# Band attention and a gated product: where P is transposed, and how two heads' scores are written

## The chip, the cores and the metric

The kernel runs on one core of one Trainium2 chip. The metric is the device time of one launch in microseconds (us), the median of a few runs.

## The reference, cut to what matters

Attention has 8 batches of 8 heads (64 heads, numbered n = 0 to 63 through all batches), each with 512 local and 32 global tokens of width 64. A local token sees the global tokens and the local ones within 32 places; a global token sees all.

```python
k_all = concatenate([k_g, k_l]); v_all = concatenate([v_g, v_l])
out_g = sm(scale * q_g @ k_all.T) @ v_all
s_ll  = where(|i - j| <= 32, scale * q_l @ k_l.T, -1e9)
out_l = sm(concatenate([scale * q_l @ k_g.T, s_ll])) @ v_all
x     = concatenate([out_g, out_l]) as (8 * 544, 512)
h     = (x @ w1) * (x @ w2)
out   = (h @ w3) @ w_out
```

All of it is float32. w3 @ w_out is folded into one matrix before it is used.

## The kernel before

**Two ways to multiply.** TensorE takes a float32 product either *plain*, in one matmul instruction that the trace shows as two records, or *split*: both operands are cut into a high part and a low part of type float32r, and two or three matmuls of those are added. Casts to high parts are made on ScalarE (ACT), the differences that give low parts on VectorE (DVE) or GpSimd (POOL). The big products (`first`, lines 816 to 818, and `second`, lines 848 to 850) are split throughout.

**A head.** Four blocks of 128 queries are taken against windows of 192 or 256 keys. `scores` (line 527) writes the four blocks into one PSUM tile `s` of two banks. `minus_max` (line 549) reads it on DVE, adds the mask and finds the maxima; `exps` on ACT makes the weights P in SBUF (two tiles, `P0` and `P1`). For the product with v, P is needed transposed, in the tile `PT` (own blocks of 128 keys, and pieces of the neighbouring blocks) and the tile `G` (global keys). `values` (line 650) then makes eight or more matmuls into two PSUM tiles, `cb` and `u` take the result out, and per pair of heads the rows are divided by their sums and become a part `x` of the rows of the big products.

**Where heads differ.** Heads 0 to 7 (`n < H`) are plain: TensorE transposes P in seven matmuls (lines 583 and 588), and the pieces are copied from PSUM. From head 8 on `PT` and `G` hold high and low parts. TensorE transposes only the four own blocks (line 583) into a PSUM tile, from which ACT takes the high parts and DVE the low. The 32-column edges and the global columns are transposed by DVE (`turn`, line 590, into `TT`), split there, and brought to their partitions by DMA: `move_edges` (lines 605 and 606, SBUF to SBUF into `PT`), `move_out` (line 611, to DRAM) and `move_in` (line 616, back into `G`). `PT` and `G` are single tiles, so these DMAs of a head start only when the values of the head before are done. Scores are plain up to head 15 (`NS = 16`): one step a head, on the 64 partitions that its half of the pair's q and k lie on. From head 16 they are split: q's two parts lie on the two halves of the partitions and k is loaded twice (lines 419 and 420), so that eight matmuls on all 128 partitions (line 546) make one head. The casts and differences for that are `prep_k` and `prep_q`.

**PSUM** has eight banks: `s` two (one buffer, also used by the global scores `sg` and the global transposes `tg`), `t0`, `t1`, `a` and `b` one each, `acc` two.

**What sets the order.** Every step has a cost by engine and a due time; the due times are the numbers of `DUE` (line 70), one a step, in the order in which the steps are listed. `list_schedule` (line 240) goes through a model of time and gives each free engine the ready step that is due first; the program is written in the order that comes out, and each engine then runs its instructions strictly in that order. All DMAs are issued by one queue, SyncE (SP), in order. `tile_orders` (line 1010) says which step must have left a buffer before the next takes it. In the middle of the program, TensorE's steps of a head stand among the matmuls of `first` and `second`, which belong to the batch before.

Of the kernel before, what the change touches and what calls it, by code (L numbers as in the profile page):

```python
# [7 lines left out]
F32 = mybir.dt.float32  # L8
# [22 lines left out]
def i(ap):  # L31
# [3 lines left out]
NX, NO, NK, NQ, MA, NS = (5, 6), 3, 3, 2, 4, 16  # L35
# [10 lines left out]
    scores32=1650, values32=(1180, 1130), gscores32=930, take=(446, 521),  # L46
# [272 lines left out]
def band_attention_glu_kernel(  # L319
# [16 lines left out]

    nc = tc.nc  # L340
    B, H = q_t.shape[0], q_t.shape[1]
    NP = H // 2
    NH = B * H
    TG = 32 * B
    S = 544

    const = ctx.enter_context(tc.tile_pool(name="const", bufs=1))
    p1 = ctx.enter_context(tc.tile_pool(name="p1", bufs=1))
# [49 lines left out]
    def load_q(n):  # L398
        b, h = divmod(n, H)
        qr = p2.tile([128, 512], F32, tag="qr", name=f"qr{n}", bufs=NQ)[0:64]  # L400
        nc.sync.dma_start(qr, q_t[b, h])
        T["qr", n] = qr
# [1074 lines left out]
```

## Time and profile before

| | |
|---|---|
| median of 3 runs | 848.13 us (847.5 to 849.35) |
| span of the profiled execution, first to last instruction | 848.0 us |
| TensorE busy | 833.2 us, 98% of the span |
| DVE, ACT, POOL busy | 67%, 63%, 45% |
| DMA engines busy | 50.1%, 129 GB/s |
| granted TensorE clock, mean | 0.996 of full speed |

The profile is of one execution of 848.0 us, 0.13 us under the median. A matmul's record reaches from its start to the end of its passage, and records overlap, so that what a step takes from TensorE is read from start to start.

### The profile page before, as it was taken

To read this page: it belongs to the slowest core of one execution; us is meant where nothing else is said; L and a number is where in the kernel's file an instruction comes from. 1 tells how busy PE (TensorE), PEld (TensorE's weight loads), DVE (VectorE), ACT (ScalarE), POOL (GpSimd) and SP (SyncE) were. 2 spreads that over 40 slices of the span, in tenths; PEclk is the share of its full clock that TensorE was granted. 3 is DMA by queue.
4 is the path that set the end of the run, shared out by engine and by line. 5 is a ranking of instruction groups with operands and counts; after the bars stand their busy time and mean duration, and the time that the engine had idled before them with its cause. 6 is when DMAs were issued, how large, how long until landed. Compare 5 with 4: busy or idle time off the path is not lost.

```text
span 848.0 us, 17752 instructions
## 1 busy us (share of the span) xinstructions
PE 833.2 (98%) x5818; PEld 750.2 (88%) x5818; DVE 567.0 (67%) x1499; ACT 536.0 (63%) x1445; POOL 383.4 (45%) x477
## 2 busy tenths in 40 slices
PE   7999999899999999999999999999999999999998
PEld 4756679799999999999999999999989999999997
DVE  5677777867777786877787767776877778531111
ACT  4666776765767786867666768676767767521111
POOL 1201455534638474747563645654755656310000
PEclk8999999999999999999999999999999999999999
DMA  9787656554647464746554554645555644200000
GB/s 292 228 250 229 183 165 165 144 129 104 147 94 170 114 158 109 170 104 165 114 137 118 131 142 121 140 116 143 123 136 123 146 97 117 50 26 2 26 18 33
DMA packets 194372, 109.75 MB, mean 129 GB/s; under 512 B 150056, under 2 KB 158504, under 8 KB 194280
## 3 DMA queue, kind: packets, MB, share of 16 engines
q1 hardware_dynamic: 194280, 108.61, 50.1%
q8 instruction: 46, 0.75, 0.4%
q14 instruction: 46, 0.38, 0.2%
HBM read 85.52 MB, written 20.28 MB: 125 GB/s over the span
## 4 chain that ended last, share of the span: by engine, by line
PE 75%; DMA 3%; SPq 1%; ACT 0%; issue 0%; POOL 0%; DVE 0%; ACTq 0%; POOLq 0%
PE acc L848 7%; PE acc L849 7%; PE ap L816 7%; PE acc L850 7%; PE bp L816 7%; PE bp L817 6%; PE ap L817 6%; PE bp L818 6%; PE ap L818 6%; PE av L665 5%; PE s L546 5%; PE t L583 3%; DMA G<-gd 2%; PE av L659 2%; PE sg L715 1%; PE s L539 1%
## 5 line engine op out<-in xcount | busy, mean ns | idle before, releaser
L816 PE MATMUL ap<-x,w12h 128*128 128x256 f32 x544 | 153.8, 283 | 0.0
L816 PE MATMUL bp<-x,w12h 128*128 128x256 f32 x544 | 153.0, 281 | 0.0
L817 PE MATMUL bp<-x,w12h 128*128 128x256 f32 x544 | 151.1, 278 | 0.0
L817 PE MATMUL ap<-x,w12h 128*128 128x256 f32 x544 | 151.0, 278 | 0.0
L818 PE MATMUL bp<-x,w12l 128*128 128x256 f32 x544 | 151.0, 278 | 0.0
L818 PE MATMUL ap<-x,w12l 128*128 128x256 f32 x544 | 150.9, 277 | 0.0
L554 ACT ACTIVATE P<-P,small 128x256 f32<-128x256 f32 (+1 forms) x256 | 121.5, 476 | 19.0 <-DVE small L550 18.7
L550 DVE CUSTOM_DVE_ANT_0 P<-s,cs 128x192 f32<-128x192 f32 (+1 forms) x256 | 88.3, 383 | 25.8 <-PE s L546 16.5
L816 PEld LDWEIGHTS ap<-x,w12h 128*128 128x128 f32 x544 | 102.3, 188 | 2.1 <-issue 0.4
L817 PEld LDWEIGHTS bp<-x,w12h 128*128 128x128 f32 x544 | 102.5, 188 | 1.1
L817 PEld LDWEIGHTS ap<-x,w12h 128*128 128x128 f32 x544 | 102.5, 188 | 1.1
L816 PEld LDWEIGHTS bp<-x,w12h 128*128 128x128 f32 x544 | 102.2, 188 | 1.4 <-issue 0.2
L818 PEld LDWEIGHTS bp<-x,w12l 128*128 128x128 f32 x544 | 102.6, 189 | 0.0
L818 PEld LDWEIGHTS ap<-x,w12l 128*128 128x128 f32 x544 | 102.4, 188 | 0.0
L679 DVE TENSOR_TENSOR u<-av,cb 64x352 f32<-64x352 f32 x112 | 57.5, 519 | 27.1 <-ACT cb L462 25.2
L465 POOL TENSOR_TENSOR kl<-kr,kh 128x608 fp32r<-128x608 f32 x37 | 56.5, 1527 | 36.9 <-ACT kh L462 26.6
L665 PE MATMUL av<-PT,vs 128*128 128x192 f32 x448 | 61.4, 263 | 0.0
L950 PE MATMUL w<-wo,w3f 128*128 128x512 f32 x128 | 60.2, 604 | 0.0
L462 ACT COPY cb<-av 64x352 f32<-64x352 f32 x93 | 41.6, 447 | 27.2 <-PE av L665 25.9
L665 PEld LDWEIGHTS av<-PT,vs 128*128 128x128 f32 x448 | 52.4, 162 | 0.7
L465 POOL TENSOR_TENSOR qs<-qr,qs 64x512 fp32r<-64x512 f32 x31 | 42.4, 1368 | 17.6 <-issue 9.3
L554 ACT ACTIVATION_READ_ACCUMULATOR P<-P,small 128x1 f32 x256 | 48.1, 188 | 0.0
(811 smaller groups left out, 2137.9 us busy)
## 6 DMA issues: line engine op xcount, KB each, us to landing
kr<-in_kd_t_dram SPq DMA_DIRECT2D x96, 152.0 KB, 3.0
raw_w<-in_w_t_dram SPq DMA_DIRECT2D x24, 512.0 KB, 4.9
kpr<-in_kp_t_dram SPq DMA_DIRECT2D x32, 272.0 KB, 3.2
out_dram<-o_None SPq DMA_DIRECT2D x33, 256.0 KB, 2.8
R<-rd SPq DMA_DIRECT2D x64, 128.0 KB, 3.2
gd<-TT SPq DMA_DIRECT2D x112, 64.0 KB, 2.7
vr<-in_v_t_dram SPq DMA_DIRECT2D x28, 256.0 KB, 3.2
G<-gd SPq DMA_DIRECT2D x112, 64.0 KB, 2.7
```

The lines of the kernel that those rows point to most:

```text
L465: (eng or nc.gpsimd).tensor_sub(dst, src, f(hi))
L550: nc.vector.tensor_tensor_reduce(blk(n, e), T["st", n][:, e, 0 : WIN[e][1]], masks[e], -0.125, 3.0e38, ALU.add, ALU.min, T["mn", n][:, e : ...
L554: nc.scalar.activation(blk(n, e), blk(n, e), AF.Exp, bias=T["mn", n][:, e : e + 1], scale=-1.0, accum_out=T["sm", n // 2][:, n % 2, e : e ...
L665: nc.tensor.matmul(av[0:r, o : o + 32 * (s1 - s0)], v[:, 0:r], PT[:, s0:s1, y, j], start=False, stop=(j % 2 == 1 and (plain or y == 1)), s ...
L679: nc.vector.tensor_add(T["u", n // 2][r : r + 64, x], T.pop(("av", n, x))[r : r + 64, 0:352], T["cb", n][r : r + 64, x])
L816: nc.tensor.matmul(d, wh[:, k, c, :], x[:, 0, 0:w], start=(k == m % 2 == 0), stop=False, skip_group_check=True)
L817: nc.tensor.matmul(d, wh[:, k, c, :], x[:, 1, 0:w], start=False, stop=False, skip_group_check=True)
L818: nc.tensor.matmul(d, wl[:, k, c, :], x[:, 0, 0:w], start=False, stop=(k == 3), skip_group_check=True)
L848: nc.tensor.matmul(a, gh[:, m % 2, sl], wh[:, c], start=(m == 0), stop=False, **part)
L849: nc.tensor.matmul(a, gh[:, m % 2, sl], wl[:, c], start=False, stop=False, **part)
L850: nc.tensor.matmul(a, gl[:, m % 2, sl], wh[:, c], start=False, stop=(m in (5, 7)), **part)
L950: nc.tensor.matmul(T["w34", t], T["w3f", t, j // 4][:, j % 4], T["wo"][:, j], start=(j == 0), stop=(j == 7))
```

## The change

Three things change, and with them every number of `DUE` (listed nowhere here).

1. Heads 8 to 15 become plain (`NF = 16` takes the place of `H` in the tests): seven TensorE transposes, plain values, no `turn` and no edge DMAs. Their global v rows lie in the plain `PT` beside those of batch 0.
2. From head 16 the four own blocks no longer pass TensorE. DVE transposes them in 32-by-32 squares (`turn_own`) into `tw`, one DMA writes that to DRAM, and four DMAs read it back into `own`, square by square in its place. The high and low parts are then made from `own`, which is in SBUF, so POOL can make them too.
3. From head 8 on the scores of a pair are one step, plain: for each block first the even head on partitions 0 to 63, then the odd one on 64 to 127, into two PSUM tiles of two banks. Within a tile the even head has one bank and the odd head the other. `load_k`, `load_q`, `prep_k` and `prep_q` are gone; k and q are loaded once a pair.

In PSUM the tags `s`, `t0` and `t1` give way to one tag `pu` with two buffers of two banks, which transposes, scores, values (from head 8), `sg` and `tg` take in turn.

```diff
     def scores(m):
+        q, k = T["q2", m], T["k2", m]
+        for h in range(2):
+            st = T["st", m, h] = ps_1.tile([128, 2, 512], F32, tag="pu", name=f"s{m}_{h}", bufs=2)
+            for e in (2 * h, 2 * h + 1):
+                o, w = WIN[e]
+                for x in range(2):
+                    r, c = slice(64 * x, 64 * x + 64), 256 * (e % 2)
+                    nc.tensor.matmul(st[:, x, c : c + w], q[r, 128 * e : 128 * e + 128], k[r, o : o + w],
+                                     start=(e % 2 == 0), stop=True, skip_group_check=True)
...
+    def turn_own(n):
+        P = Ps[n % NP_][:]
+        t = T["tw", n] = p1.tile([128, 512], F32, tag="tw", name=f"tw{n}")
+        nc.vector.transpose(view(t[:], 0, [32, 4], [128, 4], [1, 32]), view(P, 0, [256, 4], [32, 4], [1, 32]))
+
+    def own_out(n):
+        D = T["od", n] = dram.tile([128, 4, 128], F32, tag="od", name=f"od{n}", bufs=3)
+        nc.sync.dma_start(D, T.pop(("tw", n)).rearrange("p (b x) -> p b x", b=4))
+
+    def own_in(n):
+        D = T.pop(("od", n)).rearrange("(a k) b x -> b k a x", a=4)
+        L = T["own", n] = p1.tile([128, 512], F32, tag="own", name=f"own{n}")
+        for b in range(4):
+            nc.sync.dma_start(L[32 * b : 32 * b + 32].rearrange("k (a x) -> k a x", a=4), D[b])
...
     def pieces(n, e):
-        plain = n < H
+        plain = n < NF
...
+        if not plain:
+            return T["own", n].rearrange("p (a x) -> p a x", a=4), *(PT[:, 2:6, y].rearrange("p a j q -> p a (j q)") for y in range(2))
...
     def values(n, x):
-        plain = n < H
+        plain = n < NF
...
-        av = T["av", n, x] = ps_1.tile([128, 512], F32, tag="ab"[x] if plain else f"t{x}", name=f"av{x}_{n}")
+        if n < H:
+            av = ps_1.tile([128, 512], F32, tag="ab"[x], name=f"av{x}_{n}")
+        else:
+            if x == 0:
+                T["av2", n] = ps_1.tile([128, 2, 512], F32, tag="pu", name=f"av{n}", bufs=2)
+            av = T["av2", n][:, x]
...
     def tile_orders():
+        def take_s(m):
+            for h in range(2):
+                take("pu", 2, ("s", m, h), ("sp", m))
...
             else:
                 take("TT", 1, ("TT", n), ("turn", n))
+                take("own", 1, ("own", n), ("oi", n))
+                take("tw", 1, ("tw", n), ("own", n))
+                if n % 2 == 0 and n + 2 < NH:
+                    take_s(n // 2 + 1)
+                take("pu", 2, ("av", n), ("av", n, 0))
```

**The order, TensorE, scores in the middle of the program.** `s27` are the scores of head 27, `t0_26` the own transposes of head 26, `ap`, `bp` and `acc` the big products. Before:

```order
L818 MATMUL bp2_0_4_4011<-x2_3_0_3747,w12l5_998 128x256
L583 MATMUL t0_26_4076<-cs_78,P0_79 128x128 x4
L546 MATMUL s27_4081<-kh27_3877,qs27_3882 128x192
L546 MATMUL s27_4081<-kl27_3907,qs27_3882 128x192
L546 MATMUL s27_4081<-kh27_3877,qs27_3882 128x256
L546 MATMUL s27_4081<-kl27_3907,qs27_3882 128x256
L546 MATMUL s27_4081<-kh27_3877,qs27_3882 128x256
L546 MATMUL s27_4081<-kl27_3907,qs27_3882 128x256
L546 MATMUL s27_4081<-kh27_3877,qs27_3882 128x192
L546 MATMUL s27_4081<-kl27_3907,qs27_3882 128x192
L816 MATMUL ap2_0_6_4094<-x2_0_0_2765,w12h6_999 128x256
```

With the change, heads 30 and 31 (pair 15):

```order
L844 MATMUL acc2_0_128_3765<-w34h2_559,gl__3899 128x512
L515 MATMUL s15_0_3982<-kq15_3405,qp15_3408 128x192 x2
L515 MATMUL s15_0_3982<-kq15_3405,qp15_3408 128x256 x2
L515 MATMUL s15_1_3987<-kq15_3405,qp15_3408 128x256 x2
L515 MATMUL s15_1_3987<-kq15_3405,qp15_3408 128x192 x2
L810 MATMUL ap2_0_6_4003<-x2_0_0_2441,w12h6_1057 128x256
```

Eight split matmuls a head have become eight plain ones a pair, with the two heads of a block next to each other, and the own transposes are gone from TensorE.

**The order, SP, the DMAs of head 29.** `gd29` is the edge tile on its way through DRAM, `G` and `PT` what the values wait for, `od` and `own` the own blocks, `kq`, `qp`, `vr`, `kpr` loads for later heads. Before:

```order
L611 DMA gd29_4505<-TT_81 128x4x32 x2
L863 DMA out_0_dram<-o2_0_0_None_4503 128x512
L863 DMA out_0_dram<-o2_0_128_None_4508 128x512
L456 DMA vgr4_4529<-in_vg_t_dram 32x512
L457 DMA vgr4_4529<-in_vg_t_dram 32x512
L605 DMA PT1_1050<-TT_81 32x2x96
L606 DMA PT1_1050<-TT_81 32x2x96
L616 DMA G1_1045<-gd29_4505 32x16x32 x2
```

With the change:

```order
L597 DMA gd29_4048<-TT_81 128x4x32 x2
L781 DMA TGr7_4063<-gg7_3992 32x4x128 x4
L782 DMA TGg7_4064<-gg7_3992 32x4x32
L399 DMA kq17_4107<-in_kd_t_dram 128x608
L410 DMA vr15_4109<-in_v_t_dram 128x512
L416 DMA kpr17_4112<-in_kp_t_dram 128x544
L574 DMA od30_4138<-tw30_4127 128x512
L539 DMA rd15_4149<-sums_84 128x2x4
L602 DMA G1_2059<-gd29_4048 32x16x32 x2
L591 DMA PT1_2031<-TT_81 32x2x96
L592 DMA PT1_2031<-TT_81 32x2x96
L580 DMA own30_4200<-od30_4138 32x4x128 x4
```

The four DMAs on which the values of head 29 wait still stand together; more of SP's work stands between them and the edge tile's way out, and five DMAs a head (`od` and four `own`) are new.

**The order, TensorE, the first steps.** `idle` are matmuls without a use. Before:

```order
L396 MATMUL idle1_103<-vgs_82 128x256
L707 MATMUL sg0_151<-kpr0_116,QG0_112 128x272 x2
L396 MATMUL idle0_102<-vgs_82 128x256 x2
L539 MATMUL s0_170<-kq0_129,qp0_127 128x192
L539 MATMUL s0_170<-kq0_129,qp0_127 128x256 x2
L539 MATMUL s0_170<-kq0_129,qp0_127 128x192
L707 MATMUL sg1_188<-kpr1_140,QG0_112 128x272 x2
L950 MATMUL w34_0_196<-wo_99,w3f0_0_146 128x512
```

With the change:

```order
L388 MATMUL idle1_103<-vgs_82 128x256
L500 MATMUL s0_142<-kq0_114,qp0_116 128x192
L500 MATMUL s0_142<-kq0_114,qp0_116 128x256 x2
L500 MATMUL s0_142<-kq0_114,qp0_116 128x192
L701 MATMUL sg0_176<-kpr0_137,QG0_112 128x272 x2
L388 MATMUL idle0_102<-vgs_82 128x256 x2
L701 MATMUL sg1_191<-kpr1_128,QG0_112 128x272 x2
L944 MATMUL w34_0_197<-wo_99,w3f0_0_165 128x512
```

The first head's scores now stand ahead of the global ones, and the two no longer share one buffer.

## Rows read from the trace of the kernel before

**Rows 1.** The page, busy time and share of the span by engine.

```profile
PE 833.2 (98%) x5818; PEld 750.2 (88%) x5818; DVE 567.0 (67%) x1499; ACT 536.0 (63%) x1445; POOL 383.4 (45%) x477
```

**Rows 2.** Waits of PE: total us, times, longest us.

```profile
PE s L539 <- DVE small L734: 3.4, 2, 1.9
PE av L659 <- DMA G<-gd: 2.4, 6, 0.8
PE sg L707 <- DMA kpr<-in_kp_t_dram: 2.0, 1, 2.0
```

**Rows 3.** Timeline of PE, heads with split values: start us, us, what.

```profile
310.55 0.28 PE L818 MATMUL ap<-x,w12l 128*128 128x256 f32 x1
310.66 0.29 PE L659 MATMUL av<-G,vgs 128*128 128x288 f32 x1
...
311.72 0.30 PE L816 MATMUL ap<-x,w12h 128*128 128x256 f32 x1
...
313.01 0.28 PE L818 MATMUL ap<-x,w12l 128*128 128x256 f32 x1
313.12 0.25 PE L546 MATMUL s<-kh,qs 128*128 128x192 f32 x1
...
314.02 0.30 PE L816 MATMUL ap<-x,w12h 128*128 128x256 f32 x1
314.16 0.28 PE L817 MATMUL ap<-x,w12h 128*128 128x256 f32 x1
...
315.30 0.28 PE L818 MATMUL ap<-x,w12l 128*128 128x256 f32 x1
315.41 0.60 PE L583 MATMUL t<-cs,P 128*128 128x128 f32 x4
315.76 0.36 PE L816 MATMUL bp<-x,w12h 128*128 128x256 f32 x1
315.97 0.28 PE L817 MATMUL bp<-x,w12h 128*128 128x256 f32 x1
```

**Rows 4.** Timeline of PE, plain scores of one head.

```profile
124.10 0.28 PE L818 MATMUL ap<-x,w12l 128*128 128x256 f32 x1
124.31 1.78 PE L539 MATMUL s<-kq,qp 64*128 64x192 f32 x8
126.02 0.39 PE L816 MATMUL bp<-x,w12h 128*128 128x256 f32 x1
126.24 0.28 PE L817 MATMUL bp<-x,w12h 128*128 128x256 f32 x1
```

**Rows 5.** Timeline of PE, plain values and plain transposes of one head.

```profile
91.95 0.65 PE L659 MATMUL av<-G,PT 128*128 128x288 f32 x2
...
94.27 1.88 PE L950 MATMUL w<-wo,w3f 128*128 128x512 f32 x4
95.99 0.60 PE L583 MATMUL t<-cs,P 128*128 128x128 f32 x4
...
96.75 1.02 PE L950 MATMUL w<-wo,w3f 128*128 128x512 f32 x2
```

**Rows 6.** Timeline of PEld: weight loads of the first, useless matmuls.

```profile
1.18 2.21 PEld L396 LDWEIGHTS idle<-vgs 128*128 128x128 f32 x6 [1.18 <-DVE vgs L393]
4.04 1.36 PEld L396 LDWEIGHTS idle<-vgs 64*128 64x128 f32 x8 [0.65 <-issue]
```

**Rows 7.** Instructions of tile G: duration ns min/median/max, first and last start us.

```profile
L616 SPq DMA_DIRECT2D G<-gd x112: 318/479/1077, 123.6 to 739.1; - x112
...
DMA to landing us min/median/max: 2.1/2.7/5.0
```

**Rows 8.** The same of tile TT, the two edge DMAs into PT.

```profile
L605 SPq DMA_DIRECT2D PT<-TT x56: 597/643/1437, 122.2 to 737.0; - x56
L606 SPq DMA_DIRECT2D PT<-TT x56: 585/628/1171, 122.9 to 737.7; - x56
```

**Rows 9.** Groups by line, DVE: the maxima, busy us, mean ns, idle before.

```profile
L550 DVE CUSTOM_DVE_ANT_0 P<-s,cs 128x192 f32<-128x192 f32 (+1 forms) x256 | 88.3, 383 | 25.8 <-PE s L546 16.5 <-PE s L539 8.4
```

More of the change, by code (lines that the diff above doesn't have):

```diff
@@ L342, in band_attention_glu_kernel @@
     NP = H // 2
+    PB = 2
+    NF = PB * H
     NH = B * H
@@ L360, in band_attention_glu_kernel @@
     masks = [cs[:, 384:576], mask, mask, mask[:, 0:192]]
-    Ps = [const.tile([128, PW], F32, tag=f"P{e}", name=f"P{e}") for e in range(2)]
+    Ps = [const.tile([128, PW], F32, tag=f"P{e}", name=f"P{e}") for e in range(NP_)]
     TT = const.tile([128, 2, 352], F32R, tag="TT", name="TT")
@@ L524, in blk @@
     def blk(n, e):
-        return Ps[n % 2][:, PAT[e] : PAT[e] + WIN[e][1]]
-    def scores(n):
-        st = ps_1.tile([128, 4, 256], F32, tag="s", name=f"s{n}")
-        T["st", n] = st
-        T["mn", n] = minima()[:, 4 * (n % 2) : 4 * (n % 2) + 4]
-        if n % 2 == 0:
-            T["sm", n // 2] = sums[:, n // 2 % 2]
-        if n < NS:
-            rows = slice(64 * (n % 2), 64 * (n % 2) + 64)
-            q, k = T["q2", n // 2][rows], T["k2", n // 2][rows]
-            for e in range(4):
-                o, w = WIN[e]
-                nc.tensor.matmul(st[:, e, 0:w], q[:, 128 * e : 128 * e + 128], k[:, o : o + w], start=(e % 2 == 0),
-                                 stop=True, skip_group_check=True)
-            return
-        qs, kh, kl = T.pop(("qs", n)), T.pop(("kh", n)), T.pop(("kl", n))
+        return Ps[n % NP_][:, PAT[e] : PAT[e] + WIN[e][1]]
@@ L543, in scores, with scores1 @@
+    def scores1(n):
+        m, x = divmod(n, 2)
+        T["mn", n] = minima()[:, 4 * x : 4 * x + 4]
+        if x == 0:
+            T["sm", m] = sums[:, m % 2]
+        st = T["st", n] = ps_1.tile([128, 4, 256], F32, tag="pu", name=f"s{n}", bufs=2)
+        r = slice(64 * x, 64 * x + 64)
+        q, k = T["q2", m][r], T["k2", m][r]
         for e in range(4):
             o, w = WIN[e]
-            for j, kk in enumerate((kh, kl)):
-                nc.tensor.matmul(st[:, e, 0:w], qs[:, 128 * e : 128 * e + 128], kk[:, o : o + w],
-                                 start=(j == e % 2 == 0), stop=(j == 1), skip_group_check=True)
@@ L549, in minus_max, with scores @@
-    def minus_max(n, e):
-        nc.vector.tensor_tensor_reduce(blk(n, e), T["st", n][:, e, 0 : WIN[e][1]], masks[e], -0.125, 3.0e38,
+            nc.tensor.matmul(st[:, e, 0:w], q[:, 128 * e : 128 * e + 128], k[:, o : o + w], start=(e % 2 == 0),
+                             stop=True, skip_group_check=True)
+    def scores(m):
+        for x in range(2):
+            c = 4 * x
+            T["mn", 2 * m + x] = minima()[:, c : c + 4]
+        T["sm", m] = sums[:, m % 2]
+        q, k = T["q2", m], T["k2", m]
[3 more added lines that the diff above has]
+                o, w = WIN[e]
+                for x in range(2):
+                    r, c = slice(64 * x, 64 * x + 64), 256 * (e % 2)
+                    nc.tensor.matmul(st[:, x, c : c + w], q[r, 128 * e : 128 * e + 128], k[r, o : o + w],
+                                     start=(e % 2 == 0), stop=True, skip_group_check=True)
@@ L1043, in tile_orders @@
                         take("cb", 1, ("cg", k[1]), ("cg", k[1]))
[L1044 to L1047 removed]
+            take("P", NP_, ("P", n), ("mmax", n, 0))
     tile_orders()
@@ L1087, in head @@
         done = [("exps", n, e) for e in range(4)]
-        add(("t", n), only("PE", COST["transposes" if n < H else "own"]), t, done, transposes, n)
-        read(("t", n), ("P", n))
-        free = [("av", n - 1, x) for x in range(2)] if n % H or n > H else [("clear", x, b) for x in ("PT", "G")]
+        if n < NF:
+            add(("t", n), only("PE", COST["transposes"]), t, done, transposes, n)
+            read(("t", n), ("P", n))
+        free = [("av", n - 1, x) for x in range(2)] if n not in (0, NF) else [("clear", x, int(n > 0)) for x in ("PT", "G")]
@@ L1091, in head @@
         last = []
         for e, d in zip((0, 1, 2, 3, 6, 4, 5), (0.9, 1.0, 1.7, 1.3, 1.1, 1.5, 1.6)):
-            if n >= H and e in (1, 2, 3, 6):
+            if n >= NF and e in (1, 2, 3, 6):
                 continue
             h, l = ("hi", n, e), ("lo", n, e)
-            src = [("t", n)] if e not in (4, 5) else [("gw", n // 4, e - 4) if n < H else ("tgi", n // 4)]
-            add(h, hi(COST["hi"][e], 128) if e == 4 else only("ACT", COST["hi"][e]) if e == 5 else hi_psum(COST["hi"][e], COST["hi_dve"][e]), t + d, src + free, weights_hi, n, e, eng=True)
+            src = [("t", n) if n < NF else ("oi", n)] if e not in (4, 5) else [("gw", n // 4, e - 4) if n < H else ("tgi", n // 4)]
@@ L1098, in head @@
+            own = n >= NF and e == 0
+            add(h, hi(COST["hi"][e], 128) if e == 4 else only("ACT", COST["hi"][e]) if e == 5 else hi(COST["hi"][e], 512) if own else hi_psum(COST["hi"][e], COST["hi_dve"][e]), t + d, src + free, weights_hi, n, e, eng=True)
             d += 0.8
-            tile_ = ("TG", n // 4) if e in (4, 5) else (f"t{int(e > 0)}", n)
+            tile_ = ("TG", n // 4) if e in (4, 5) else ("own", n) if own else ("t", n)
             read(h, tile_)
-            if e not in (4, 5):
-                held[h] = tile_
@@ L1103, in head @@
-            if n >= H:
-                add(l, either(None, (COST["lo"][e], COST["lo"][e])) if e else only("DVE", COST["lo"][e]), t + d, [h], weights_lo, n, e, eng=True)
+            if e not in (4, 5) and not own:
+                held[h] = (f"t{int(e > 0)}", n)
+            if n >= NF:
+                add(l, either(None, (COST["lo"][e], COST["lo"][e]) if e else COST["ownl"]), t + d, [h], weights_lo, n, e, eng=True)
                 read(l, tile_)
-                if e == 0:
-                    held[l] = tile_
@@ L1108, in head @@
-            last.append(l if n >= H else h)
-        if n >= H:
+            last.append(l if n >= NF else h)
+        if n >= NF:
             add(("turn", n), only("DVE", COST["turn"]), t, [*done, ("clear", "vgs")], turn, n)
             read(("turn", n), ("P", n))
+            add(("own", n), only("DVE", COST["ownt"]), t + 0.2, done, turn_own, n)
+            read(("own", n), ("P", n))
+            add(("oo", n), dma(450), t + 1.0, [("own", n)], own_out, n, nbytes=262144)
+            read(("oo", n), ("tw", n))
+            add(("oi", n), dma(450, 450, 450, 450), t + 3.0, [("oo", n)], own_in, n, nbytes=300000)
@@ L1131, in head @@
                     [me, *[("sum", n, 0)] * x], values_take, n, x, eng=True)
-                read(("sum", n, x), (f"av{x}", n), ("u", n // 2))
+                read(("sum", n, x), (f"av{x}", n) if n < H else ("av", n), ("u", n // 2))
                 continue
@@ L1163, in pair_values @@
         take("vr", 1, ("vr", m), ("load", "v", m))
-        add(("load", "v", m), dma(450, *[450] * (m < NP)), t - 14.0, (), load_pair, m, nbytes=262144)
-        if m < NP:
+        add(("load", "v", m), dma(450, *[450] * (m < PB * NP)), t - 14.0, (), load_pair, m, nbytes=262144)
+        if m < PB * NP:
             return
@@ L1235, in batch @@
             add(("load", "qg", 0), dma(650, 650), t - 45.0, [("clear", "QG", 0)], load_qg0, nbytes=65536)
-            add(("load", "vg", 0), dma(650), t - 12.0, [("clear", "PT", 0)], load_vg0, nbytes=65536)
-            read(("load", "vg", 0), ("PT", 0))
+            for c in range(PB):
+                add(("load", "vg", c), dma(650), t - 12.0 + 40.0 * c, [("clear", "PT", 0)], load_vg0, c, nbytes=65536)
+                read(("load", "vg", c), ("PT", 0))
             read(("load", "qg", 0), ("QG", 0))
@@ L1376, in band_attention_glu_kernel @@
         for b in range(2):
-            add(("clear", x, b), only("POOL", ns), base(H) - (30.0 if x == "QG" else 6.0) if b else due, (), fresh, x, b)
+            add(("clear", x, b), only("POOL", ns), (base(H) - 30.0 if x == "QG" else base(NF) - 6.0) if b else due, (), fresh, x, b)
     add(("clear", "vgs"), only("POOL", 952), 0.0, (), fresh_vgs)
```

168 lines of the change are left out of this document (73 added, 95 removed), and 322 rows, old and new, of the table DUE.

## The prediction

> **What bounds the kernel now.** I read the page first: TensorE is busy in 98% of the span, DVE, the next, in 67% [rows 1]. Then the waits of TensorE: they come to less than 10 us in all, most of it before the first heads have their data (the scores of the first heads wait 3.4 us for the maxima that free their PSUM tile, the global scores 2.0 us for their keys), and 2.4 us in six waits later, where values wait for the edge tile G [rows 2]. So the kernel is as long as TensorE's list of work. What a step adds to that list I read in the timeline from start to start, since a record's length overlaps the next.
>
> Between products of the big matrices, two slots of which take 0.23 us, the own transposes of a head cost 315.97 - 315.30 - 0.23 = 0.44 us; they include a later start of the product behind them [rows 3]. The split scores of a head cost 314.16 - 313.01 - 0.23 = 0.92 us, the split values 311.72 - 310.55 - 0.11 = 1.06 us [rows 3]. The plain scores of one head cost 126.24 - 124.10 - 0.23 = 1.91 us, of which 1.71 us are the matmuls and 0.2 us the slots at both sides [rows 4]. The plain values cost 94.27 - 91.95 = 2.32 us and the seven plain transposes 96.75 - 95.99 = 0.76 us [rows 5]; to the latter I add the 0.09 us by which transposes delay a product (0.21 instead of 0.11 to 0.12 us behind them [rows 3]), 0.85 us.
>
> **The change part by part.**
>
> *Heads 8 to 15 plain.* Transposes 8 x (0.85 - 0.44) = +3.3 us; values 8 x (2.32 - 1.06) = +10.1 us. Against that, their eight steps of scores at 1.91 us go: -15.3 us. The edges' transposes on DVE, their casts and the edge DMAs of eight heads go too. They lie beside TensorE's work and I cost their going at nothing.
>
> *Own blocks off TensorE, heads 16 to 63.* 48 x 0.44 = -21.1 us. Instead DVE gets a third transpose a head and SP five DMAs. DVE is idle in a third of the span [rows 1] and loses all its low parts of k and q, ACT loses 96 casts and the low parts of the own blocks may go to POOL. So these engines end up with no more work than before, and I cost it at nothing on the path. The cover is the distance between a pair's scores and its values: in the new order there are two heads' values and some 20 us of TensorE's work between them. If that were short, the values would be late instead.
>
> *Scores of a pair in one plain step, heads 8 to 63.* The split scores of heads 16 to 63 go: 48 x 0.92 = -44.2 us. There come 28 steps at a price p that the trace does not show. If the two heads of a block, on the two halves of the partitions, run beside each other, a step takes what one head takes: p = 1.91 us [rows 4]. If one head runs after the other, p = 2 x 1.71 + 0.2 = 3.6 us. The nearest row is that of the matmuls without a use at the start: eight weight loads on half the partitions, with the halves in turn, take 1.36 us together, six loads on all partitions 2.21 us [rows 6]. One after the other at the latter pace the eight would take 2.9 us; so the halves go side by side there. That stretch runs at a slower pace than the later ones (2.21 / 6 = 0.37 us a load, where two products with their loads take 0.23 us), so that later the instructions come faster one behind the other; for this I add 0.1 us and take p = 2.0: +56.0 us. All above but the 28 steps is 3.3 + 10.1 - 15.3 - 21.1 - 44.2 = -67.2 us; with them it is -11.2 us. With p = 1.91 it is -13.7, with p = 3.6 it is +33.6; the sum is zero at p = 2.4.
>
> The Trainium skill (TensorE: Matmul & The Clock Gate, Measured speedup) gives less than full gain for packed rows: 3.07 times for four row tiles. An estimate by that page, the same 77% of the ideal for two, would give p = 2 x 1.71 / 1.53 + 0.2 = 2.4 us and a sum of about zero. By that page nothing would be left of the saving; the row above shows no such loss, at its slower pace, and no row here shows it at the later one.
>
> *The new place of the scores in PSUM.* A pair's scores take both buffers of `pu`, and the values of the next head need one of them, which is free when four maxima are taken. A maximum is 0.38 us [rows 9], four of them 1.5 us; the new order leaves about 5 us of products or more behind the scores in the middle of the program. I cost it at nothing, as long as DVE takes the maxima at once.
>
> *The start.* The first scores no longer wait for the tile of the global ones. At most the 3.4 + 2.0 us of the two waits go [rows 2]; but the fold products behind need their weights, which come by the same queue in nearly the same order, so I take -1 us, between -5 and +2.
>
> *The edges.* The values of a head wait for four DMAs that may start only when the values of the head before are done. With medians: two into PT, 0.64 + 0.63 us of issue, two into G, 2 x 0.48 us, small gaps, and 2.7 us to landing, 5.1 us in all (4.5 us with the fastest landing) [rows 7, 8]. From the new order, with a product counted as 0.115 us and one of `second` as 0.23 us, the work between the values of two heads is 4.5 us twice (heads 29 and 45), 5.1, 5.2 and 5.4 us once, and 5.9 or 6.1 us eight times; before the change it was 6.3 us and more but for one place at the end. So two or three heads wait about 0.6 us, and spread adds some: +1.5 us to the waits of 2.4 us that there are [rows 2].
>
> *Sum.* -11.2 - 1 + 1.5 = -10.7 us against the 848.0 us of the profiled execution: **837.3 us**. The median of the runs shown is 0.13 us above it; I predict **837.4 us**.
>
> **The rivals.**
>
> *A. The edges come too late: slower.* Per head, five DMAs come to SP and about two go, for 1.5 us more of issue at half a microsecond each; and more of them stand ahead of the edges in the queue, which is strictly in order. If SP comes to the first edge DMA L us after the values' end, the chain of 5.1 us becomes 5.1 + L; for the 13 heads with 6.1 us or less (72.1 us together) the waits are 13 x (5.1 + L) - 72.1. At L = 2 they are 20 us: 848.0 - 11.2 - 1 + 20.2 = **856 us**. It decides from L = 1.4, where the saving is eaten. For it: the six waits for G show that this chain touches TensorE already [rows 2]. Against: the low parts of k and q, on which loads in the same queue waited, are gone, and at the tight places the four DMAs stand together in the new order.
>
> *B. The halves run beside each other in part or not at all: no gain, or much slower.* With half of the overlap p is (1.91 + 3.6) / 2 = 2.75 us, the sum -67.2 + 28 x 2.75 = +9.8 us and the time 848.0 + 9.8 + 0.5 = **858 us**; with none it is 848.0 + 33.6 + 0.5 = **882 us**. For it stands only that no row shows a pair at the later pace; against it the weight loads [rows 6]. The Trainium skill's figure above would stand between, at about 848 us.
>
> *C. The waits move into PSUM's two buffers.* If each of the 24 pairs' next values waits 0.45 us for the maxima, 10.8 us are given back: **848 us**, no change. For it: the maxima had 25.8 us of idle time before them, mostly for scores, so DVE follows scores closely only when it is not behind with other work [rows 9]. Against: 5 us against 1.5 us.
>
> *D. More than forecast.* p at its lower bound, the start's two waits gone, no more waits at the edges: -13.7 - 5 = **829 us**.
>
> **How the numbers follow.** The forecast case (830 to 846 us, with p from 1.9 to 2.2 and waits up to some 5 us) gets 0.72, A 0.10, B 0.05, C 0.08, D 0.05. About 0.2% (1.7 us) is what a measurement of this kernel tells from no change. Faster by more: the forecast and D, 0.77. Within it: most of C and a little of A and B, 0.09. Slower: the rest, 0.14. The range takes in D below and the first part of A above, so far that no more than 2 in 10 is outside: 828 to 852 us.
>
> **What would show it.** In the profile of the changed kernel, right: no transposes of own blocks on TensorE from head 16; a pair's scores taking 1.8 to 2.0 us from the last product before to the first behind; values of heads 8 to 15 at 2.3 us; TensorE's busy share still about 98%, with waits for G below 5 us. Wrong: pairs of 2.4 us or more (B); a row of waits of PE for G or PT in total over 12 us (A), or for the maxima on scores, values and `sg` (C); DVE's or SP's chain of waits in the middle of the program.

## The result, and the profile after

The changed kernel takes **839.12 us** (median of 4 runs, 836.66 to 840.28) against 847.82 us (847.42 to 849.35) of the kernel before on the same chip: ratio 0.989, with a 95% interval of 0.9869 to 0.9912. Forecast were 837.4 us, between 828 and 852. The profiled execution has a span of 838.1 us, 9.9 us less than the 848.0 us of before; its time as a run was 839.91 us, so that 1.8 us lie outside the span. The forecast saving was 10.7 us; the spans differ by 9.9 and the medians by 8.7.

The page of the changed kernel, busy time and share of the span by engine, answers to [rows 1]:

```profile
PE 821.3 (98%) x5666; PEld 728.7 (87%) x5666; DVE 525.6 (63%) x1436; ACT 480.5 (57%) x1354; POOL 327.4 (39%) x429
```

TensorE still sets the time, with 12 us less of busy time, and DVE, ACT and POOL have less to do as well; only SP's queue has more, of which more below. Its waits (total us, times, longest us) answer to [rows 2]:

```profile
PE sg L701 <- issue: 6.7, 1, 6.7
PE av L653 <- DMA G<-gd: 3.3, 5, 1.3
```

The waits for G are 3.3 us in place of 2.4; no wait for maxima or for a buffer of `pu` has a row of any size. The 6.7 us are one wait at the start, of which more below. The steps that changed, in the timeline of TensorE (start us, us, what): first a pair's plain scores in the middle, then the plain values of the tenth head, one of batch 1:

```profile
404.53 0.28 PE L812 MATMUL ap<-x,w12l 128*128 128x256 f32 x1
404.74 1.78 PE L515 MATMUL s<-kq,qp 64*128 64x192 f32 x16
406.45 0.38 PE L810 MATMUL ap<-x,w12h 128*128 128x256 f32 x1
406.67 0.28 PE L811 MATMUL ap<-x,w12h 128*128 128x256 f32 x1
```

```profile
133.99 0.65 PE L653 MATMUL av<-G,PT 128*128 128x288 f32 x2
134.47 0.87 PE L659 MATMUL av<-PT,vr 128*128 128x192 f32 x4
135.18 0.59 PE L653 MATMUL av<-G,PT 128*128 128x256 f32 x2
135.61 0.87 PE L659 MATMUL av<-PT,vr 128*128 128x224 f32 x4
136.18 0.42 PE L709 MATMUL sg<-kph,QG 128*128 128x272 f32 x1
```

Sixteen records of two heads take 406.45 - 404.74 = 1.71 us, as long as eight of one head did [rows 4]; the step costs 406.67 - 404.53 - 0.23 = 1.91 us. These plain values cost 136.18 - 133.99 = 2.19 us; over the eight heads that became plain, all plain values together grew by 18.2 us from start to start, 2.27 us a head.

### The profile page after: what moved, and what is told of

Its sections match the earlier page's. It is cut to its first block, busy times and chain, and to the rows that moved or that the text cites. A ratio compares the mean times of both kernels' runs of the same rounds, so it can differ in the third digit from the quotient of the medians.

```text
span 838.1 us, 17284 instructions
## 1 busy us (share of the span) xinstructions
PE 821.3 (98%) x5666; PEld 728.7 (87%) x5666; DVE 525.6 (63%) x1436; ACT 480.5 (57%) x1354; POOL 327.4 (39%) x429
## 4 chain that ended last, share of the span: by engine, by line
PE 88%; DMA 4%; SPq 3%; DVE 2%; issue 1%; ACT 1%; POOL 0%; ACTq 0%; DVEq 0%; POOLq 0%
PE bp L810 7%; PE ap L810 7%; PE acc L842 7%; PE av L659 7%; PE bp L811 7%; PE bp L812 7%; PE acc L844 7%; PE ap L811 7%; PE acc L843 7%; PE ap L812 7%; PE w L944 7%; PE s L515 5%; PE av L653 3%; PE s L500 1%; DMA G<-gd 1%
## 5 line engine op out<-in xcount | busy, mean ns | idle before, releaser
L528 ACT ACTIVATE P<-P,small 128x192 f32<-128x192 f32 (+1 forms) x256 | 121.1, 474 | 15.6 <-DVE small L524 14.9
L524 DVE CUSTOM_DVE_ANT_0 P<-s,cs 128x256 f32<-128x256 f32 (+1 forms) x256 | 85.0, 385 | 4.2 <-PE s L515 2.7
L673 DVE TENSOR_TENSOR u<-av,cb 64x352 f32<-64x352 f32 x96 | 49.2, 520 | 46.3 <-ACT cb L441 45.1
L441 ACT COPY cb<-av 64x352 f32<-64x352 f32 x77 | 34.4, 447 | 59.0 <-PE av L659 51.7
L444 POOL TENSOR_TENSOR PT<-own,PT 128x512 fp32r<-128x512 f32 x36 | 48.1, 1337 | 32.1 <-ACT PT L441 23.1
L659 PE MATMUL av<-PT,vs 128*128 128x192 f32 (+3 forms) x384 | 52.8, 264 | 0.4 <-DMA PT<-TT 0.4
L515 PE MATMUL s<-kq,qp 64*128 64x192 f32 (+1 forms) x448 | 50.0, 362 | 0.0
L515 PEld LDWEIGHTS s<-kq,qp 64*128 64x128 f32 x448 | 39.2, 186 | 8.8 <-issue 2.2
```

The source lines that it names most:

```text
L515: nc.tensor.matmul(st[:, x, c : c + w], q[r, 128 * e : 128 * e + 128], k[r, o : o + w], start=(e % 2 == 0), stop=True, skip_group_check=True)
L524: nc.vector.tensor_tensor_reduce(blk(n, e), s, masks[e], -0.125, 3.0e38, ALU.add, ALU.min, T["mn", n][:, e : e + 1])
L528: nc.scalar.activation(blk(n, e), blk(n, e), AF.Exp, bias=T["mn", n][:, e : e + 1], scale=-1.0, accum_out=T["sm", n // 2][:, n % 2, e : e ...
L659: nc.tensor.matmul(av[0:r, o : o + 32 * (s1 - s0)], v[:, 0:r], PT[:, s0:s1, y, j], start=False, stop=(j % 2 == 1 and (plain or y == 1)), s ...
L673: nc.vector.tensor_add(T["u", n // 2][r : r + 64, x], T.pop(("av", n, x))[r : r + 64, 0:352], T["cb", n][r : r + 64, x])
```

## The experiments

The theory: TensorE's list of work sets the time, the two heads of a pair run on the two halves of the array side by side, and the DMAs that replace the own transposes have room. Rivals: the halves overlap only by the order in which their instructions stand; the transposes were hidden anyway; SP is close to setting the edges (rival A). Two things in the trace were not foreseen and got runs of their own: the slow start, and a slower pace of the big products.

**The order of a pair's scores.** Two runs keep the work and change only which instruction follows which.

```diff
-            for e in (2 * h, 2 * h + 1):
-                o, w = WIN[e]
-                for x in range(2):
+            for x in range(2):
+                for e in (2 * h, 2 * h + 1):
+                    o, w = WIN[e]
```

> Within each PSUM tile of a pair's scores both blocks of the even head are written first, then both of the odd head; all else stays. Theory 'the two halves of the partitions run beside each other, and TensorE starts its instructions in order': only at a change of head can two instructions overlap, so that eight slots of 0.43 us (1.71 us / 4) end as five in place of four, p = 1.91 + 0.43 = 2.3 us, and the time rises by 28 x 0.43 = 12 us to about 851 us. Rival 'a change of head empties the array first, the overlap holds only for instructions of one shape issued pairwise': p = 3.6 us, +47 us, about 886 us. Rival 'it is no overlap, a matmul on half the partitions is short by itself': p stays 1.9 us, 839 us.

Measured: 839.9 us in one run, no change to see. In the timeline the step takes 405.12 - 403.31 = 1.81 us:

```profile
403.31 1.89 PE L515 MATMUL s<-kq,qp 64*128 64x192 f32 x16
405.12 0.39 PE L810 MATMUL ap<-x,w12h 128*128 128x256 f32 x1
```

28 x 0.10 = 2.8 us of cost in place of 12, 47 or 0. The time is that of the third expectation, "no overlap", but the trace speaks against it. In its first 0.1 us the step has two records already (the same timeline, cut at 403.40 us):

```profile
403.31 0.44 PE L515 MATMUL s<-kq,qp 64*128 64x192 f32 x2
```

The starts of the records tell what the first expectation had wrong. A plain matmul has two records, and the program has 192, 256 columns of the even head, then 192, 256 of the odd one. In the trace of all 28 steps the first four records to start are 192 columns wide: the odd head's first block starts ahead of the even head's second. So a matmul for the other half of the array starts past one that still waits for its own half, and what was said above, that each engine runs its instructions strictly in order, does not hold for TensorE across the two halves. The Trainium skill (TensorE: Matmul & The Clock Gate, The mechanism) lets weight loads be pulled ahead, but says that matmuls start and end strictly in their order; this trace disagrees as to their start. How far that reaches, the next run asked:

```diff
+        for x in range(2):
+            for e in range(4):
...
+                nc.tensor.matmul(T["st", m, e // 2][:, x, c : c + w], q[r, 128 * e : 128 * e + 128], k[r, o : o + w],
+                                 start=(e % 2 == 0), stop=True, skip_group_check=True)
```

> Of a pair's scores all four blocks of the even head are written first, then all four of the odd one. With two and two in turn a step still took 1.82 us of matmuls in place of 1.71, not the 2.1 us that a start in strict order gives. Theory 'each half of the array has its own line of waiting instructions, several deep': the odd head's instructions still start while the even head's wait, and a step takes at most 0.3 us more than 1.71, 28 x 0.3 = 8 us, 840 to 848 us. Rival 'only about two instructions are looked ahead': two blocks of the even head run alone before the odd one can begin, 2 x 0.43 us more a step, +24 us, about 864 us. Rival 'no overlap is left': 3.4 us a step, +48 us, about 888 us.

Measured: 858.32 us, and in the timeline

```profile
412.02 2.64 PE L515 MATMUL s<-kq,qp 64*128 64x192 f32 x16
414.60 0.38 PE L810 MATMUL ap<-x,w12h 128*128 128x256 f32 x1
```

a step takes 2.58 us, 0.87 us more, or two blocks of 0.43 us, as the second expectation has it. How far one half gets past the other is seen in the same step, cut at 412.86 and at 412.90 us:

```profile
412.02 1.02 PE L515 MATMUL s<-kq,qp 64*128 64x192 f32 x4
412.02 1.29 PE L515 MATMUL s<-kq,qp 64*128 64x192 f32 x6
```

For 0.84 us only the two records each of the even head's first two blocks start, while the other half has nothing to do. Then the even head's third block starts, and 6 ns behind it a record 192 columns wide, the odd head's first block; all 28 steps have this order. When the even head's second block started, two of its blocks still stood before the odd head's first; now one does. So a matmul for the other half passes one waiting block, and not two.

28 x 0.87 = 24 us, but the time, of one run, is only 17 us over the 841.6 us of the repeat below. The big products, the values and the global scores took 8 us less from start to start; 5 us of these are idle time that the longer steps covered (behind the first big product TensorE is idle for 2.5 us in place of 7.3), the rest is not explained. So the overlap is real: it can be lost in part, and that costs. The order of the change, head by head within a block, is well inside its reach.

**The transposes put back on TensorE.**

```diff
         g0 = 64 if x else 0
+        if not plain and x == 0:
+            for _ in range(4):
+                nc.tensor.transpose(av[:, 384:512], ident, ident)
```

> Ahead of the values of each head from 16 on, TensorE makes four 128x128 transposes of the identity into columns of the values' PSUM tile that nobody reads; the output stays the reference's. Theory 'TensorE's list of work sets the time': the 21.1 us that the own transposes were put down with come back (48 x 0.44), less what falls into waits for G (3.3 us in all): 839 + 18 to 21 = 857 to 860 us. Rival 'the transposes lay beside other work, and the gain came from the scores alone': within 4 us of 839.

Measured: 854.56 us, 13.0 us over the changed kernel in the same set (841.6 us, below). Before the values of a head stands

```profile
397.08 0.28 PE L815 MATMUL ap<-x,w12l 128*128 128x256 f32 x1
397.20 0.60 PE L655 MATMUL av<-cs 128*128 128x128 f32 x4
397.55 0.38 PE L656 MATMUL av<-G,vgs 128*128 128x288 f32 x1
397.77 0.57 PE L662 MATMUL av<-PT,vs 128*128 128x192 f32 x4
```

0.35 us of transposes, and 0.22 in place of 0.13 us behind them: 0.44 us. Summed from start to start, the values' matmuls with the transposes take 21.8 us more than in the repeat, which is the 21.1 of the forecast. The rival, under which the time would not have moved by more than 4 us, is out: the transposes were on the path. But the time, of one run, stays under the expected 857 to 860 us, as the big products took 9.0 us less than in the repeat (all `ap`, `bp` and `acc`, start to start). In part the transposes cover waits: behind the first big product TensorE is idle for 2.6 us in place of 7.3. In part the products have a faster pace, which is the next subject.

**The pace of the big products.** In the last 100 us, where TensorE has hardly anything else, 24 products take 761.25 - 758.43 = 2.82 us with the change, 117.5 ns each, and 763.18 - 760.46 = 2.72 us before it, 113.3 ns each. Timeline with the change, then before:

```profile
758.43 0.28 PE L810 MATMUL bp<-x,w12h 128*128 128x256 f32 x1
...
761.25 0.40 PE L842 MATMUL acc<-w34h,gh__9795 128*128 128x512 f32 x1
```

```profile
760.46 0.28 PE L816 MATMUL bp<-x,w12h 128*128 128x256 f32 x1
...
763.18 0.28 PE L816 MATMUL ap<-x,w12h 128*128 128x256 f32 x1
```

The last 650 instructions of TensorE are 500 products and 150 `acc` in both kernels, and nothing else. Their windows (time in the window, busy us and instructions of PE, PEld, DVE, ACT, POOL, then granted clock, DMA share, GB/s), with the change, then before:

```profile
742.04:834.81 92.77, 92.31 (x651) 86.16 (x650) 16.34 (x24) 17.00 (x30) 1.48 (x2) 1.00 0.04 14
```

```profile
754.03:843.93 89.90, 89.90 (x651) 84.25 (x650) 17.09 (x25) 15.81 (x28) 1.49 (x2) 1.00 0.04 13
```

They take 2.9 us more, of which 0.5 us is one wait and 2.4 us the pace. In the middle both paces occur in both kernels; with the change the slower one is more frequent, and a product that stands between products takes 115.4 ns on average in place of 115.1. With `acc` that is about 1 us. First the kernel as it is:

> The changed kernel as it is, profiled once more. In its first profile a product of the big matrices takes about 118 ns in the last 100 us, in the kernel before about 114 ns. Theory 'a state of the run': the pace differs from execution to execution, and this profile shows the last 100 us at about 114 ns at least in part, with a span some 3 to 5 us shorter than 838.1 us. Rival 'a property of the program': 118 ns there again and a span within 1 us of 838.1. Time by both: 836 to 841 us.

Measured: 841.6 us (840.64 to 842.93), ratio 0.9907 (0.9886 to 0.9927), span 840.4 us, and 117.8 ns again in the last 100 us. So the theory of a state of the run is out and the pace belongs to the program: the last 650 instructions take 92.78 us again. The span is 2.3 us longer for another reason, as far as the waits tell: values wait 1.1 and 0.9 us for DVE at two places that have no wait in the first profile. Then two shifts of TensorE's program, by one split and by one plain useless matmul:

```diff
         idle_products(IDLE[None])
+        nc.tensor.matmul(T["idle"][0][:, 0:32], vgs[:, 0], vgs[:, 0, 0, 0:32], start=True, stop=True)
```

> One more useless matmul in split type, 32 columns wide, stands among the useless ones at the start, so that all later instructions of TensorE lie two instructions (a weight load and a matmul) further on in its program; it ends before the first data are there. Four profiles of the order without it show about 117.8 ns a product in the last 100 us; the kernel before and the one with the useless transposes show about 114. Theory 'the pace hangs on where the instructions lie': the last 100 us go to another pace, at 114 ns the whole takes some 3 to 5 us less, 835 to 838 us. Rival 'the pace hangs on what TensorE did before, and the transposes set it right': 117.8 ns in the last 100 us again and 839 to 842 us.

```diff
         idle_products(IDLE[None])
+        idle_products(((0, 128, 32),))
```

> The same with one plain useless matmul, 32 columns wide, which shows as two records: the later instructions lie four further on, if a record is an instruction. Theory 'where the instructions lie': the pace of the last 100 us changes here or with the shift by two, or both; at 114 ns 835 to 838 us. Rival 'what TensorE did before': 117.8 ns and 839 to 842 us, here and there.

Measured: 844.54 and 840.29 us, one run each, 117.8 ns in both. Where the instructions lie is not the cause, for these two shifts. The first time lies above both ranges; why is not known. Next, whether it is kept from the last scores:

```diff
+        if n == NH - 1 and x == 0:
+            for _ in range(4):
+                nc.tensor.transpose(av[:, 384:512], ident, ident)
```

> Once in the whole program, ahead of the values of head 63, TensorE makes four 128x128 transposes of the identity into columns that nobody reads. All profiles of the changed order show a product at 117.8 ns from there to the end, and in the first of them the same pace of 117 to 119 ns goes back without a break to the last pair's scores at 693 us, ahead of which it was 113 to 114. Theory 'the array is left in a slower rhythm by the pair's scores, and keeps it until other work breaks it': behind the four transposes the products run at about 114 ns to the end, 2 to 3 us less for the last 100 us, 836 to 840 us. Rival 'the last 100 us have this pace for another reason': 117.8 ns again, 839 to 842 us.

```diff
+        if not plain and x == 0 and n % 2 == 0:
+            nc.tensor.transpose(av[:, 384:512], ident, ident)
```

> One useless 128x128 transpose of the identity ahead of the values of every even head from 16 on, which are the first values behind a pair's scores: 24 in all, at about 0.11 to 0.2 us each, 3 to 5 us of work more. Theory 'kept rhythm, and one transpose breaks it': the pace of products goes from 115.5 to about 114.5 ns in the middle and from 117.8 to 114 in the last 100 us, some 7 us less for products and acc together, so that the whole takes 2 to 4 us less than the change, 836 to 838 us, ratio about 0.987. Rival 'a single transpose does not break it, it took four': the 3 to 5 us come on top, 842 to 846 us.

Measured: 842.39 us, and 841.03 us (839.47 to 841.77; ratio 0.9904, 0.9885 to 0.9924), 117.8 ns in the last 100 us of both. In the second run the values take 4.5 us more than in the repeat, but the time is not longer, so that it lies between the two ranges that were expected. Behind the one set of transposes, 15 products take 734.90 - 733.13 = 1.77 us, 118 ns each:

```profile
731.25 0.60 PE L655 MATMUL av<-cs 128*128 128x128 f32 x4
...
733.13 0.28 PE L813 MATMUL ap<-x,w12h 128*128 128x256 f32 x1
...
734.90 0.40 PE L845 MATMUL acc<-w34h,gh__9519 128*128 128x512 f32 x1
```

My theory of a kept rhythm that a transpose breaks has fallen in this form. What is left: the pace goes by stretches, changes at other work, and is the same at the end in all three profiles of the change; with the transposes of every head the fast one is back, with one set or with one each second head it is not. In the run with more DMAs, below, it is fast at the end without any (816.19 - 813.47 = 2.72 us for 24 products), and there TensorE has the very instructions of the change in the same order. So TensorE's own program does not settle the pace by itself. Its cause stays open.

**SP's load.**

```diff
         for b in range(4):
-            nc.sync.dma_start(L[32 * b : 32 * b + 32].rearrange("k (a x) -> k a x", a=4), D[b])
+            for g in range(2):
+                to = L[32 * b : 32 * b + 32, 256 * g : 256 * g + 256].rearrange("k (a x) -> k a x", a=2)
+                nc.sync.dma_start(to, D[b][:, 2 * g : 2 * g + 2])
```

> The own blocks of heads 16 to 63 come back by eight DMAs of half the size in place of four: 48 x 4 = 192 more issues, at half a microsecond each 2 us a head and 96 us in all on SP. Theory of the prediction 'SP has room, and the edges' DMAs stand together': the waits of values for G and PT stay under 10 us in all (3 us now), 839 to 847 us. Rival A 'SP is nearly what sets the edges': L grows by up to 2 us on the 13 tight heads, the waits go to 20 us and more, 856 us or later.

Measured: **898.67 us** in one run, 57 us over the repeat of the change. The expectation by the prediction's theory was wrong by far, and rival A's direction right. The page, the waits of PE, and the own blocks' DMAs (duration ns min/median/max, first and last start us):

```profile
PE 841.4 (94%) x5666; PEld 739.5 (82%) x5666; DVE 519.0 (58%) x1436; ACT 481.9 (54%) x1354; POOL 320.9 (36%) x429
```

```profile
PE av L655 <- DMA G<-gd: 32.6, 17, 3.7
PE av L655 <- POOL G L444: 3.3, 3, 2.5
```

```profile
L582 SPq DMA_DIRECT2D own<-od x384: 302/425/2322, 207.9 to 783.9; - x192
```

192 x 0.425 = 82 us more of issue on SP lengthen the span by 896.9 - 838.1 = 59 us. TensorE is idle for 896.9 - 841.4 = 55 us in place of 17, with 17 waits for G of up to 3.7 us, and its own work takes 20 us more. In part that is the clock: its mean granted value is 0.981 in place of 0.995, so that it was at its lower level, half of full speed, for about 2 x 0.019 x 897 = 34 us in place of 8. The transfers themselves are hardly slower: from issue to landing the DMAs into G take 2.5 us (median) in place of 2.4, those into `own`, of half the size, 1.9 in place of 2.5. In the changed kernel SP's issues between 200 and 700 us add up to 376 of 500 us, before the change to 329 (759 and 621 DMAs, summed over their records). At 75% this queue, which issues in order and has its own waits between, had little left. So the change works with SP near its bound, which the 3.3 us of waits for G do not tell.

**The start.** The timeline of the changed kernel's first 20 us (in brackets the idle time before, and what ended it):

```profile
5.17 1.67 PE L500 MATMUL s<-kq,qp 64*128 64x192 f32 x8
13.56 2.15 PE L701 MATMUL sg<-kpr,QG 128*128 128x272 f32 x4 [6.72 <-issue]
15.51 1.91 PE L388 MATMUL idle<-vgs 128*128 128x256 f32 x4
17.21 1.50 PE L701 MATMUL sg<-kpr,QG 128*128 128x272 f32 x4
18.55 1.02 PE L944 MATMUL w<-wo,w3f 128*128 128x512 f32 x2
```

The keys of pair 0 are loaded behind those of pair 1, and the fold (`w`, the folding of w3 and w_out) begins at 18.55 us (16.10 before). Two runs:

```diff
+        done = list_schedule(steps, after, held)
+        at = {steps[n][0]: j for j, (_, n, _) in enumerate(done)}
+        j, k = at["load", "kp", 0], at["load", "kp", 1]
+        done[j], done[k] = done[k], done[j]
```

> At the start the loads of the keys of pair 0 and pair 1 change places in SP's queue; no other instruction moves. In the changed kernel the first global scores wait 6.7 us for the keys of pair 0, DVE waits for those scores ahead of the first weights, and the first fold product starts at 18.55 us (16.10 before the change). Theory 'the order of these loads cost the start': the global scores run at about 8 us, the fold starts 2 to 3 us earlier, and the time falls by as much, to 836 to 837 us. Rival 'the fold waits for its weights, which come by the same queue': the fold starts within 1 us of 18.55 and the time stays 838 to 840 us.

Measured: 840.27 us (839.23 to 842.81), ratio 0.9896 (0.9874 to 0.9918); the repeat of the change in the same set had 841.6. The theory holds at first: the first global scores start at 7.83 us and the fold at 16.55 us, 2.0 us earlier. Then most of the gain is gone: the first big product starts at 117.95 us, against 118.41 in the repeat, and the times do not differ clear of noise. The windows of 3 us (columns as above) show half clock from 15 to 18 us and beyond:

```profile
12.00:15.00 3.00, 1.20 (x3) 0.99 (x4) 2.26 (x11) 2.30 (x10) 0.00 (x0) 0.73 1.03 387
15.00:18.00 3.00, 2.41 (x5) 0.91 (x4) 2.58 (x8) 2.15 (x5) 0.00 (x0) 0.50 1.11 251
18.00:21.00 3.00, 3.00 (x11) 2.08 (x10) 1.69 (x6) 1.17 (x5) 0.00 (x0) 0.64 0.96 359
```

This is nothing that the change brought. The kernel before has the same half clock there, behind two waits of 1.9 and 2.0 us with one head's scores between them:

```profile
12.00:15.00 3.00, 1.00 (x3) 0.76 (x3) 2.56 (x11) 2.41 (x9) 0.00 (x0) 0.60 0.96 297
15.00:18.00 3.00, 3.00 (x6) 1.49 (x6) 1.52 (x6) 1.35 (x6) 0.00 (x0) 0.50 1.10 351
18.00:21.00 3.00, 2.93 (x15) 2.10 (x13) 2.25 (x6) 1.87 (x6) 0.00 (x0) 0.76 1.08 388
```

So, with the keys swapped, the gap was filled with useless matmuls:

```diff
-("sg", 0): ((0, 128, 256), (0, 128, 256),)}
+("sg", 0): ((0, 128, 256),) * 10, ("sg", 1): ((0, 128, 256),) * 3}
```

> The order of the key loads as in the run with keys swapped, and eight more useless 128x256 matmuls behind the first global scores and three more behind the second, which fill the gap in which TensorE waits for keys and weights. There TensorE ran at half clock from about 12 to 19 us, behind a gap of some 4 us, and the work that came earlier took twice its time: the fold began 1.6 us sooner, but the first big product only 0.46 us sooner. Theory 'the half clock ate the gain of the earlier keys': with no gap the clock stays at its upper level, global scores take 1.2 in place of 2.15 us, two fold matmuls 1.0 in place of 2.0, the first big product starts 1.5 to 3 us earlier, at 115 to 116.5 us, and the time is 837 to 839 us. Rival 'the weights come no sooner, TensorE only waits at other places': the first big product stays within 0.7 us of 117.95 and the time is 839.5 to 842 us.

> The changed kernel once more as it is, beside the run with more useless matmuls on one chip, for a closer interval of the change itself: by its own time and the repeat before, 839 to 842 us, ratio 0.989 to 0.991 to the kernel before. A pace of 117.8 ns in the last 100 us once more, if it belongs to the program.

Measured: 840.48 us (837.71 to 844.52; ratio 0.9887, 0.9858 to 0.9916) and, for the change once more, 841.5 us (838.69 to 843.04; 0.989, 0.9867 to 0.9913), as expected, with 117.8 ns again. With the gap filled the clock stays at its upper level,

```profile
12.00:15.00 3.00, 2.98 (x15) 2.27 (x14) 2.21 (x9) 2.64 (x10) 0.00 (x0) 1.00 1.03 389
15.00:18.00 3.00, 2.50 (x13) 1.39 (x11) 2.76 (x7) 2.00 (x6) 0.00 (x0) 1.00 1.15 279
```

and the first big product starts at 115.76 us against 119.13 in the run beside it:

```profile
115.76 0.68 PE L810 MATMUL ap<-x,w12h 128*128 128x256 f32 x1
```

```profile
119.13 0.68 PE L810 MATMUL ap<-x,w12h 128*128 128x256 f32 x1
```

That is 3.4 us for the swapped keys and the filled gap together; the filled gap alone brings 117.95 - 115.76 = 2.2 us, within the 1.5 to 3 us of the theory of the half clock, which is right at its place; but the time lies in the range of the rival. Of the 3.4 us the spans keep 1.2 (838.3 against 839.5) and the medians 1.0; the intervals overlap widely, so no version is shown to be faster than the change. The rest is lost behind the first big product, 0.7 us of it as idle time of TensorE (7.0 against 6.3; 1.4 us of values behind a difference on DVE is its longest wait). Where the remainder went the profile does not tell.

## Why the prediction was right, step by step

- **TensorE's list of work bounds the kernel: right.** Busy share 98% again. Work put back on TensorE came out as time, if not in full: 13 us for 21.8 us of transposes, 17 us for 24 us of overlap lost in the pairs. About 5 us in each run went into waits that were there already.
- **Scores of a pair: right, p a little too high.** Taken as 2.0 us, measured 1.91, the lower bound: 28 x 0.09 = 2.5 us more gain. The 0.1 us that was added for the later, faster pace was not needed. Rival B is out; the estimate from the Trainium skill's figure for four row tiles (TensorE: Matmul & The Clock Gate, Measured speedup), by which p would have been 2.4 us and the time about 848, does not hold for two halves here: 1.71 us for two heads, 1.71 us for one.
- **Plain values of heads 8 to 15: right.** +10.1 us forecast, +10.0 in the sum of all values from start to start; 2.32 us a head forecast, 2.27 measured.
- **Own transposes: right**, 21.1 us forecast, 21.8 us of TensorE's time by the run that put them back.
- **PSUM: right.** No waits for `pu` or the maxima; rival C did not occur.
- **The edges: right in size, wrong in what was said for it.** +1.5 us forecast, +0.9 measured. But "they stand together at the tight places" is not room: rival A, with 0.10, was at most four DMAs a head away from deciding. Its working in the prediction, waits of 13 tight heads, gave 20 us at L = 2; the run with 1.7 us more of issue a head (4 x 0.425) gave 57. What it left out: 17 heads waited for G and not 13, TensorE was idle for 38 us more, and its work took 20 us more, in part at the lower clock.
- **The start: wrong in its mechanism, small in size.** "The first scores no longer wait" is true (5.17 us), but the wait moved to the global scores behind, 6.7 us. At the first big product the change is 119.14 - 118.77 = 0.4 us ahead, with -1 forecast; its two other profiles have 118.41 and 119.13 us there.
- **Not in the sum: the pace of products.** It was taken as the same before and after. With p = 1.91 the sum for the work is -13.7; with -0.4 at the start and +0.9 at the edges it would be -13.2, and the spans differ by -9.9, so that 3.3 us were given back. By its size the pace accounts for them: 2.4 us in the last 650 instructions and about 1 us in the middle. That the pace is the price of this change is not shown, as its cause is open.
- **So the nearness is in part luck.** Two errors of opposite sign, 2.5 us in p and 3.3 us in the pace, leave the forecast within 2 us of the measured time.

## What to carry to other kernels

Scores on half the partitions were nearly free here beside those on the other half: read the cost of a pair from what one half takes, and let the two halves take turns, one instruction and one. Before moving work from a busy engine to a DMA round trip, add up the issues of the queue: at three quarters of its time this queue, which issues in order, showed 3 us of waits, and 82 us more of issue cost 57. Work that is pulled into a stretch at half clock takes twice as long there, so look at the granted clock before counting a gain at the start; and a gain at the start is a gain in time only if nothing behind it waits.

## What the runs showed of the hardware

- A plain matmul on one half of the array starts past one earlier matmul that waits for the other half, and not past two (a step takes 1.71 us with one and one in turn, 1.82 us with two and two, 2.58 us with four and four).
- The same stream of split products has two steady paces, 113 and 118 ns, at a granted clock of 1.00 in both. In the slower one every third weight load lasts 192 in place of 188 ns. The last 650 instructions take 92.78 us in all eleven profiles with the slower pace to the end, of nine programs in the order of the change, and 90.58 us in the two programs with the faster one (four transposes ahead of every head's values, eight DMAs for the own blocks). What chooses is open.
- At the start the granted clock fell from 1.00 to 0.50, its lower level of 1.2 GHz: with the change in 6.7 us without a matmul, in the kernel before in the second of two waits, of 1.9 and 2.0 us with one head's scores between them. At the lower level four records of global scores took 2.15 us and the first two fold matmuls 2.05 (keys swapped); with the gap filled the clock stayed at 1.00 and they took 1.16 and 1.10 us.
